# Attention and channel mix on one core: mu by DMA, value weights behind batch 1's loads, more unread matmuls, last tile in halves, new places for the steps

**Chip, cores, metric.** One core of one Trainium2 chip. The metric is the time of one execution in microseconds, device time. A program on one core has no die to compare with, so "fast" only says that no run lay over 1.5% above the fastest of its kernel.

## The reference, cut to what matters

```python
# attention over 32 memory slots; 8 batches, 8 heads, 576 tokens, 64 per head
a = softmax(phi, axis=tokens)
k_m, v_m = a^T k, a^T v                       # per head: 32 x 64
attn = softmax(q k_m^T / 8);  x = attn v_m    # heads side by side: 576 x 512
# channel mix
xk = mu_k * x + (1 - mu_k) * x_prev;  xr = mu_r * x + (1 - mu_r) * x_prev
out = sigmoid(xr @ w_r) * (relu(xk @ w_k) ** 2 @ w_v)
```

Inputs and output are float32. The kernel multiplies in bf16; the load from memory casts.

## The kernel before: what the change touches

The work of a batch is cut into named steps: q0 to q3 transpose queries, k, v and z are the products with exp(phi), nk and nv their norms, s0 to s3 scores, l0 to l3 logs of the denominators, mk and mr the mixing products. Channel mix runs in nine chunks of 512 tokens, 16 groups each: eight of keys, four gates, four of values. A list gives each step a place, counted in groups, and the places settle every engine's order. (A suffix such as +pv names the result buffer that the step borrows; digits after an underscore are only a label.) In the traces an engine's work comes in that order, and a step that waits holds up what stands behind it: in the kernel before TensorE stood idle for 3.09 us until batch 0's keys landed, and for 1.89 us at 50 us until VectorE had weights.

```python
FIRST = {0: [("exp", -36), ("busy16_572686", -36), ("k+pv", -34), ("z", -32), ..., ("mu", -26), ("s1", -25), ...],
         1: [...], 2: [...], 3: [...]}        # later batches: STEADY
ORDER = ('wv', 'phi', 'k', 'q', 'v')          # loads after those of batch 0 and w_k, w_r
# ... cut ...
    mu_row = const.tile([1, 2, Dm], F32, name="mu_row")
    nc.sync.dma_start(out=mu_row[:, 0], in_=moe_mu_k.unsqueeze(0))
    nc.sync.dma_start(out=mu_row[:, 1], in_=moe_mu_r.unsqueeze(0))
# ... cut: the step "mu" ...
        for jj in range(2):                   # mu_row to all partitions, by TensorE
            nc.tensor.matmul(ps[jj * 64:(jj + 1) * 64], lhsT=ones_f, rhs=mu_row...[:, :, :, jj, :], ...)
        for w in range(2):
            nc.vector.tensor_mul(mu_m[:, w, 0], mask, ps[:, w])
            nc.vector.tensor_sub(mu_m[:, w, 1], mask, mu_m[:, w, 0])
# ... cut: a group of values ...
                o = work.tile([128, Dm], F32, name="o", tag="o", bufs=2)
                for fi in range(NF):
                    nc.tensor.matmul(pv, lhsT=st["sq"][:, fi, ts * 128:(ts + 1) * 128],
                                     rhs=wv_sb[:, fi, :], start=(fi == 0), stop=(fi == NF - 1))
                nc.vector.tensor_mul(o, st[ts // 2][:, ts % 2], pv)
                store(o, t0 // 128 + ts)
```

"busy16" is 16 matmuls on zeros whose result nobody reads: they are meant to keep TensorE's clock up. All loads that cast go through one queue, issued by GpSimd, in program order.

The softmax here doesn't subtract the row's maximum and nothing guards it: scores larger than these inputs give would overflow.

## Time and profile before

| | before |
|---|---|
| time, median of 3 runs (range) | 235.5 us (235.37 to 235.9) |
| span of the profiled run | 233.9 us |
| first keys matmul | 25.48 us |
| stretch bound by TensorE's work | from about 76 us to 228.8 us |

The page's engine rows for PE and for its clock. Columns of the first row: busy us, share, instructions; the second row is the granted clock in tenths in 40 slices of 5.8 us.

```profile
PE 215.5 (92%) x1606; PEld 107.6 (46%) x1633; DVE 142.1 (61%) x353; ACT 162.1 (69%) x305; POOL 54.0 (23%) x74
...
PEclk9956799999999999999999999999999999999999
```

### The profile page before, as it was taken

To read this page: it belongs to the slowest core of one execution; us is meant where nothing else is said; L and a number is where in the kernel's file an instruction comes from. 1 tells how busy PE (TensorE), PEld (TensorE's weight loads), DVE (VectorE), ACT (ScalarE), POOL (GpSimd) and SP (SyncE) were. 2 spreads that over 40 slices of the span, in tenths; PEclk is the share of its full clock that TensorE was granted. 3 is DMA by queue.
4 is the path that set the end of the run, shared out by engine and by line. 5 is a ranking of instruction groups with operands and counts; after the bars stand their busy time and mean duration, and the time that the engine had idled before them with its cause. 6 is when DMAs were issued, how large, how long until landed. Compare 5 with 4: busy or idle time off the path is not lost.

```text
span 233.9 us, 4281 instructions
## 1 busy us (share of the span) xinstructions
PE 215.5 (92%) x1606; PEld 107.6 (46%) x1633; DVE 142.1 (61%) x353; ACT 162.1 (69%) x305; POOL 54.0 (23%) x74
## 2 busy tenths in 40 slices
PE   7398798869998999999999999999999999999991
PEld 3234345445435445445544684454444444444440
DVE  3254743387566778588657856786577877525222
ACT  3107478761799595889698959895988865765760
POOL 8672155545524607300810000000000000000000
PEclk9956799999999999999999999999999999999999
DMA  7999999999999999993499400320023033023034
GB/s 141 187 200 206 239 192 231 191 259 216 254 209 163 169 227 258 180 189 129 115 163 211 97 3 0 90 93 0 3 91 90 1 90 93 0 91 90 0 69 113
DMA packets 48633, 31.23 MB, mean 134 GB/s; under 512 B 14826, under 2 KB 42994, under 8 KB 48612
## 3 DMA queue, kind: packets, MB, share of 16 engines
q0 software_dynamic: 41520, 20.91, 63.9%
q1 hardware_dynamic: 6932, 9.78, 14.4%
q8 instruction: 13, 0.21, 0.4%
q10 hardware_dynamic: 160, 0.26, 0.3%
q14 instruction: 8, 0.07, 0.1%
HBM read 38.28 MB, written 9.44 MB: 204 GB/s over the span
## 4 chain that ended last, share of the span: by engine, by line
PE 81%; ACT 5%; DMA 4%; DVE 3%; issue 2%; SPq 1%; POOL 1%; DVEq 0%; POOLq 0%
PE pk L483 25%; PE pv L513 23%; PE pr L497 13%; PE qtps L295 4%; PE kvps L241 4%; DMA q<-in_q_dram 3%; PE scps L309 2%; PE nops L349 2%; PE zps L322 2%; SPq L464 1%; PE mxps L403 1%; DMA out_dram<-o 1%; PE mxps L407 1%; PE zps L251 1%; DVE o L515 1%
## 5 line engine op out<-in xcount | busy, mean ns | idle before, releaser
L483 PE MATMUL pk<-xkT,wk 128*128 128x512 bf16 (+1 forms) x309 | 66.9, 360 | 1.2 <-issue 0.5
L513 PE MATMUL pv<-wv,sq 128*128 128x512 bf16 x280 | 65.1, 379 | 0.6 <-issue 0.2
L487 ACT ACTIVATE rl<-pk 128x512 bf16<-128x512 f32 x72 | 43.1, 601 | 25.4 <-PE pk L483 23.7
L488 DVE TENSOR_TENSOR sq<-rl 128x512 bf16<-128x512 bf16 x72 | 29.9, 423 | 25.9 <-ACT rl L487 25.9
L515 DVE TENSOR_TENSOR o<-sg,pv 128x512 f32<-128x512 f32 x36 | 23.9, 686 | 35.5 <-ACT sg L505 27.8
L483 PEld LDWEIGHTS <-wk 128*128 128x128 bf16 x320 | 29.6, 98 | 28.1 <-issue 1.2
L513 PEld LDWEIGHTS <-sq 128*128 128x128 bf16 x288 | 27.8, 98 | 31.7
L497 PE MATMUL pr<-wr,xrT 128*128 128x512 bf16 x137 | 34.9, 380 | 0.4 <-issue 0.2
L502 ACT ACTIVATE sg<-pr 128x512 f32<-128x512 f32 x36 | 21.7, 604 | 10.5 <-PE pr L497 10.5
L312 ACT ACTIVATE e<-scps 128x288 bf16<-128x288 f32 x32 | 11.7, 431 | 12.2 <-PE scps L309 12.2
L497 PEld LDWEIGHTS <-xrT 128*128 128x128 bf16 x144 | 13.0, 98 | 15.4 <-issue 1.4
L504 ACT ACTIVATE sg<-sg 128x1024 f32<-128x1024 f32 x18 | 19.0, 1057 | 0.6
L505 ACT ACTIVATE sg<-sg 128x1024 f32<-128x1024 f32 x18 | 19.0, 1057 | 0.6
L353 ACT CAST x<-nops 128x288 bf16<-128x288 f32 x48 | 16.6, 413 | 0.0
L374 DVE TENSOR_SCALAR mu_d<-diff,mu 128x576 bf16<-128x576 bf16 x48 | 15.6, 368 | 0.0
L299 DVE COPY qT<-qtps 128x576 bf16<-128x576 bf16 x32 | 12.9, 450 | 4.3 <-PE qtps L295 4.2
L295 PE MATMUL qtps<-identity,q 128*64 128x128 bf16 x320 | 12.9, 233 | 1.9 <-DMA q<-in_q_dram 0.7
L324 ACT ACTIVATE lz<-zps 128x288 f32<-128x288 f32 x32 | 12.0, 415 | 3.8 <-PE zps L322 3.8
L109 POOL DMA_DIRECT2D phm<-in_phi_dram x7 | 6.3, 895 | 36.1 <-ACT em L225 31.6
L241 PE MATMUL kvps<-kv,em 128*64 128x256 bf16 (+1 forms) x200 | 10.8, 255 | 3.2 <-DMA kv<-in_k_dram 3.1
L336 DVE TENSOR_TENSOR atn<-e,lz 128x576 bf16<-128x576 bf16 x16 | 11.9, 753 | 1.9 <-ACT lz L329 1.8
L295 PEld LDWEIGHTS <-q 128*64 128x64 bf16 x320 | 10.4, 116 | 4.8 <-issue 3.0
(70 smaller groups left out, 214.1 us busy)
## 6 DMA issues: line engine op xcount, KB each, us to landing
out_dram<-o SPq DMA_DIRECT2D x38, 128.0 KB, 2.4
kv<-in_k_dram POOLq DMA_DIRECT2D x8, 512.0 KB, 10.4
out_dram<-o SPq DMA_DIRECT2D x16, 256.0 KB, 4.8
phm<-in_phi_dram POOLq DMA_DIRECT2D x7, 512.0 KB, 10.7
q<-in_q_dram POOLq DMA_DIRECT2D x7, 512.0 KB, 11.7
kv<-in_v_dram POOLq DMA_DIRECT2D x7, 512.0 KB, 12.1
wk<-in_moe_w_k_dram POOLq DMA_DIRECT2D x2, 512.0 KB, 9.8
wv<-in_moe_w_v_dram POOLq DMA_DIRECT2D x1, 1024.0 KB, 16.8
```

Of the source, the lines that this page charges most:

```text
L241: nc.tensor.matmul(kvps[jj * 64:(jj + 1) * 64, c], lhsT=heads(j, pr * 64, 64), rhs=kv5[:, parts, 2 * pr:2 * pr + 2, j, :], start=j == 0 an ...
L295: nc.tensor.matmul(ps[i * D:(i + 1) * D, j * 128:(j + 1) * 128], lhsT=q5[:, 2 * pr + i, j, :], rhs=identity, is_transpose=True, start=True ...
L353: nc.scalar.copy(st["x"][:, 2 * c + jj, sl], pss[jj])
L483: nc.tensor.matmul(pk[:, lo:hi], lhsT=wk_sb[:, di, fi * 128:(fi + 1) * 128], rhs=xk_T[:, di, c0:c0 + hi - lo], start=(di == 0), stop=(di = ...
L487: nc.scalar.activation(rl, pk, AF.Relu)
L488: nc.vector.tensor_mul(st["sq"][:, fi, :], rl, rl)
L497: nc.tensor.matmul(pr, lhsT=xr_T[:, di, c0:c0 + 128], rhs=wr_sb[:, di, :], start=(di == 0), stop=(di == ND - 1))
L502: nc.scalar.activation(sg[:, ts % 2], pr, AF.Exp, scale=-1.0)
L504: nc.scalar.activation(sg, sg, AF.Ln, bias=1.0)
L505: nc.scalar.activation(sg, sg, AF.Exp, scale=-1.0)
L513: nc.tensor.matmul(pv, lhsT=st["sq"][:, fi, ts * 128:(ts + 1) * 128], rhs=wv_sb[:, fi, :], start=(fi == 0), stop=(fi == NF - 1))
L515: nc.vector.tensor_mul(o, st[ts // 2][:, ts % 2], pv)
```

## The change

The intent: shorten the way to the first keys matmul (mu by DMA, fillers until the keys land), have batch 1's keys and queries there sooner, and shorten the end. With it came new places for most steps, which its description does not name. The diff, cut to its core:

```diff
-    0: [("exp", -36), ("busy16_572686", -36), ("k+pv", -34), ..., ("mu", -26), ("s1", -25), ...
+    0: [("exp", -58), ("busy23_232748", -54), ("mu", -48), ("k+pv", -47), ("z+pv", -45), ("busy1_400335", -45), ...
     (nearly all places of batches 0 to 3 and some steady ones; 9 fillers in later waits instead of 4)
-ORDER = ('wv', 'phi', 'k', 'q', 'v')
+ORDER = ('phi', 'k', 'q', 'wv', 'v')
-    nc.scalar.preload_act_table_set("natural_log_exp_and_others")      # moved behind the four issues
+    mu_b = const.tile([128, 2, 2, 2 * D], F32, name="mu_b")
+    for w, mu in enumerate((moe_mu_k, moe_mu_r)):
+        for jj in range(2):
+            nc.scalar.dma_start(out=mu_b[jj * 64:(jj + 1) * 64, w],
+                in_=mu.rearrange("(c j x) -> j c x", c=2, j=2)[jj:jj + 1].to_broadcast([64, 2, 2 * D]))
-            nc.tensor.matmul(ps[jj * 64:(jj + 1) * 64], lhsT=ones_f, ...)
-            nc.vector.tensor_mul(mu_m[:, w, 0], mask, ps[:, w])
+            nc.vector.tensor_mul(mu_m[:, w, 0], mask, mu_b[:, w])
-                o = work.tile([128, Dm], F32, name="o", tag="o", bufs=2)
+                o = work.tile([128, Dm], F32, name="o", tag="o", bufs=3)
+                n = 2 if c == NCH - 1 and ts == 3 else 1        # product and store by halves of the columns
```

## The prediction

The table load that part 1 speaks of took 1.28 us from 0.74 us on.

> **What bounds the kernel now.** I read the page's slices first, then stretches of time, then the order of instructions of the first 60 us, then the end. The stretches were cut at every 3.41 us up to 31 us, because the granted clock turned out to flip on that grid. The columns are: stretch, its length, busy us of TensorE's matmuls, its weight loads, VectorE, ScalarE and GpSimd (instructions in brackets), granted clock, DMA share, GB/s.
>
> ```profile
> 4.10:7.51 3.41, 2.10 (x10) 0.89 (x9) 0.98 (x13) 1.40 (x2) 3.33 (x7) 1.00 1.44 183
> 7.51:10.92 3.41, 1.08 (x30) 0.90 (x29) 0.47 (x3) 0.00 (x0) 1.79 (x3) 0.99 1.62 188
> 10.92:14.33 3.41, 3.26 (x27) 1.61 (x27) 1.50 (x6) 0.00 (x0) 2.63 (x4) 0.50 1.56 192
> 17.74:21.15 3.41, 3.39 (x26) 1.38 (x26) 0.74 (x2) 2.75 (x8) 0.88 (x1) 0.51 1.25 206
> 21.15:24.56 3.41, 1.73 (x40) 1.14 (x38) 3.09 (x8) 1.70 (x5) 1.43 (x2) 0.99 1.24 207
> 24.56:27.97 3.41, 3.08 (x25) 1.32 (x21) 2.28 (x7) 1.76 (x4) 0.14 (x1) 0.51 1.19 263
> 36.00:48.00 12.00, 10.71 (x130) 6.08 (x130) 4.52 (x12) 9.20 (x17) 6.29 (x8) 1.00 1.51 212
> 48.00:60.00 12.00, 9.68 (x138) 6.07 (x135) 10.19 (x28) 5.13 (x12) 6.31 (x8) 1.00 1.42 239
> 76.00:150.00 74.00, 73.26 (x577) 39.12 (x583) 53.29 (x129) 58.84 (x118) 16.23 (x21) 1.00 0.85 141
> 150.00:222.00 72.00, 71.47 (x396) 32.95 (x403) 44.79 (x100) 54.41 (x94) 0.00 (x0) 1.00 0.19 56
> ```
>
> From 76 us to the last matmul (228.8 us) TensorE is idle for 0.74 + 0.53 + 0.08 = 1.35 us at full clock, and eight 512-column matmuls take 1.73 us, 216 ns each. No part of the change removes work there, so those 153 us stay. All that can be won lies in four places: the time until the first key matmul, which comes at 25.48 us; the half clock around it; idle TensorE between 28 and 76 us (0.05 + 1.29 + 2.32 + 0.77 = 4.4 us); and the 5.1 us after 228.8 us.
>
> The way to 25.48 us is a chain of latencies, shown by these lines of the timeline (start, duration, engine, line, what; in brackets the idle time before):
>
> ```profile
> 1.19 5.01 PE L193 MATMUL idle<-zeros 128*128 128x512 bf16 x16 [1.19 <-DVE zeros L137]
> 9.29 0.75 PE L241 MATMUL kvps<-kv,em 128*64 128x128 bf16 x20 [3.09 <-DMA kv<-in_k_dram]
> 11.07 1.35 PE L295 MATMUL qtps<-identity,q 128*64 128x128 bf16 x20 [0.69 <-DMA q<-in_q_dram]
> 12.88 1.97 PE L203 MATMUL psmu<-mu_row,ones_f 1*64 1x512 f32 x4
> 14.78 0.45 PE L309 MATMUL scps<-qT,kmT 128*64 128x288 bf16 x2
> 20.14 0.69 ACT L329 ACTIVATE lz<-lz 128x576 f32<-128x576 f32 x1
> 25.48 1.49 PE L483 MATMUL pk<-xkT,wk 128*128 128x512 bf16 x3 [0.33 <-DVE xkT L412]
> 50.07 0.30 PE L403 MATMUL mxps<-atn,vm 64*128 64x288 bf16 x2 [1.89 <-DVE atn L336]
> 229.28 0.69 DVE L515 TENSOR_TENSOR o<-sg,pv 128x512 f32<-128x512 f32 x1 [0.42 <-DMA out_dram<-o]
> ```
>
> Keys land at 9.2 us, the first queries at 11.0. The broadcast of mu on TensorE occupies it from 12.88 to 14.85 us, just where the first score matmul (14.78) could go. The first reciprocal is at 20.14. The last output product has 0.42 us of wait for a store to free one of two buffers.
>
> [...] with clock shares solved for the instant of change, the flips lie at 10.84, 21.08, 24.52 and 27.92 us, multiples of 3.41 us apart, and the filler matmuls go from 430 to 216 ns apart after 4.1 us. [...] the stretch 10.92 to 14.33 is busy 3.26 of 3.41 us, with 22 transposes and four one-row matmuls in it, and the next one was not granted full clock. [...]
>
> **Part 1: mu by DMA.** Removed: 1.97 us of TensorE, which delays the first scores, and the 0.47 us that the third query transpose waits for a buffer which mu held. Moved: the four mask operations (0.42 us each, 1.7 us together) from 14.9 to 16.5 us on VectorE into its idle time before the keys (7 to 10.4 us). Added: four issues on ScalarE's queue, at the 0.25 to 0.56 us of the small issues on SP some 1.8 us; the table load then ends near 4 us, and phi lands at 5.3: hidden. Also added: 4 x 128 rows of 512 B = 512 packets. The page's queue table gives 63.9% of 16 x 233.9 us for 41520 packets, 58 ns each, so 512 of them cost 16 engines 1.8 us. [...] I estimate that keys and queries come 0.5 us later, not 1.8.
>
> Now the chain. VectorE's order becomes: first query copy, keys' norm, second copy, key transpose copy. From queries at 11.07: transposes at full clock 0.47 (ten later in the trace), copy 0.45 to 12.0, norm 0.61 to 12.65, copy to 13.1, key copy 0.28 to 13.4; first scores at 13.4 instead of 14.78. Then, with the durations of the trace: exponentials 0.41 + 0.35 to 14.55; third query pair 14.55 to 15.0 and fourth 15.55 to 16.0 on VectorE, two logs meanwhile; third and fourth exponential 16.4 to 17.1; first reciprocal at 17.1 instead of 20.14, because mu's masks and the half clock no longer sit between. Weights (0.75) to 18.6, masked values (four, 1.13) to 19.75, second weights to 20.5, last mixing matmuls about 21, their copies on two engines to 22.3; first keys matmul about 21.9, as its first pieces start before the last copy. With 0.5 us of later keys: 22.4. **Gain: 25.48 - 22.4 = 3.1 us**; I count 2.9.
>
> **Part 2: unread matmuls.** 23 instead of 16 before the keys: 7 x 0.216 = 1.5 us more, so they end near 7.7 us, where TensorE is idle until 9.3. In all 9 other ones instead of 4 lie in later waits. They cost nothing there, and should hold the clock. Before, from 25.48 to 27.97 TensorE worked at half rate, a loss of 1.2 us. [...] **Expected gain: 0.45 us**, out of 1.2 won or 0.8 lost.
>
> **Part 3: value weights behind phi, keys and queries of batch 1.** The value weights write 1 MB; at the measured 200 GB/s that is 5.2 us. Batch 1's phi, keys and queries land 5 us sooner, the value weights later. They landed at 12.04 + 16.8 = 28.8 us and were first read at 41.3, so there was room. In the new order they land near 37 us (where batch 1's queries landed before), and the first value matmul comes at 22.4 + 12 groups of 0.863 + mixing 0.7 + batch 1's keys, sums, queries and scores 3.7 = 37.2 us: just in time. Without this part the earlier start would run into late queries. Batch 1's scores now stand one group earlier, so that a value group lies between scores and weights; of the waits (1.89 for weights, 0.46, 0.57) I expect half to go. **Gain: 0.8 us** net of some wait on the value weights.
>
> **Part 4: last tile in halves, third output buffer.** The matmul work is the same. The last gate's chain on ScalarE still ends at 227.08 + 1.06 = 228.14 us; then 0.69 for the tile before, then two halves at an estimated 0.38: 229.65 instead of 229.97. The last store moves half the bytes, but sits behind another issue of about 0.5 us on its queue. **Gain: 0.4 us.**
>
> Sum: 2.9 + 0.45 + 0.8 + 0.4 = 4.55; I take off a little for the new order of the steady steps, which has nothing to win: 235.5 - 4.3 = **231.2 us**, 1.8% faster.
>
> **Rivals.** A: the broadcast delays keys. For it: the keys are the first thing that TensorE waits for (3.1 us)[...]. [...] If its 1.8 us came in full, 1.3 us more is lost: 232.5. B: a new wait on the value weights or on phi takes back the head start[...]. For it: my two times differ by 0.2 us. Against: the swap takes out exactly the 5 us item in front. It would give 233. C: the clock fails, half rate from 22.4 to 27.9, 2.7 us lost instead of 1.2: 233. D: [...] most of batch 1's waits go: 229.5.
>
> **Range and chances.** A, B and C are each perhaps one in four and rarely together; D is one in five. I put 229.2 to 233.4 at 8 in 10. The border of 2% is 230.8, only 0.4 below my number: faster 0.42, same 0.56, slower 0.02, since a loss of 4.7 us would need a stall that nothing in the profile suggests.
>
> **What would show it.** Right: first scores near 13.9 us, first keys matmul at 22 to 23, clock 1.00 from there on, idle TensorE between 28 and 76 us below 4 us, the last matmul near 224.5, the last output product not waiting for a store, and the steady stretch as long as before. Wrong: keys' first matmul after 10.2 us (A); a wait of value matmuls on a DMA near 38 us or of ScalarE on phi near 28 (B); clock 0.5 in the stretch after the first keys matmul (C); or a change of some us in the steady stretch, which would break the premise that it is bound by TensorE's work alone.

## The result

The changed kernel takes 232.68 us (median of 4 runs, 232.32 to 233.43), the kernel before 235.44 us in the same rounds. The ratio is 0.9887, interval 0.9855 to 0.9919: the same at a threshold of 2%, though clear of 1. Ratios here are the mean time of one kernel's fast runs over that of the other's of the same rounds, so not quite the ratio of the medians.

The same two rows of the page, after:

```profile
PE 217.9 (94%) x1649; PEld 108.4 (47%) x1649; DVE 142.6 (62%) x353; ACT 161.2 (70%) x305; POOL 54.1 (23%) x74
...
PEclk9958999999999999999999999999999999999998
```

The change adds 16 matmuls by count of its parts (12 fillers and 8 for the halves, less 4 records of mu), and 1649 less 16 is 1633. So the profile of before lacks 27 matmul records, and a missing record looks like an idle TensorE.

The order of the first 64 us, after (timeline: start, duration, engine, line, what; idle time before in brackets), with the lines that answer to those of before:

```profile
10.11 0.87 PE L238 MATMUL kvps<-kv,em 128*64 128x128 bf16 x20 [1.60 <-DMA kv<-in_k_dram]
...
12.05 0.75 PE L292 MATMUL qtps<-identity,q 128*64 128x128 bf16 x10 [0.50 <-DMA q<-in_q_dram]
...
14.77 0.69 PE L306 MATMUL scps<-qT,kmT 128*64 128x288 bf16 x4 [0.43 <-DVE kmT L282]
...
23.25 2.96 PE L480 MATMUL pk<-xkT,wk 128*128 128x512 bf16 x12
...
50.92 0.81 PE L292 MATMUL qtps<-identity,q 128*64 128x128 bf16 x22 [0.44 <-DMA q<-in_q_dram]
...
63.53 0.68 PE L292 MATMUL qtps<-identity,q 128*64 128x128 bf16 x10 [0.50 <-DMA q<-in_q_dram]
```

Keys come 0.82 us later than before and queries 0.98 us; yet the keys matmuls start 2.2 us earlier. New are waits of TensorE on queries at 50 and 63 us.

And the stretches (length, busy us of matmuls, weight loads, VectorE, ScalarE, GpSimd, clock, DMA share, GB/s), cut where this run's clock flipped:

```profile
8.37:11.78 3.41, 1.59 (x32) 1.14 (x32) 1.99 (x6) 0.00 (x0) 1.42 (x2) 1.00 1.65 188
11.78:15.20 3.42, 2.72 (x27) 1.63 (x29) 1.63 (x5) 0.00 (x0) 2.40 (x4) 0.50 1.58 191
15.20:18.61 3.41, 3.41 (x31) 1.65 (x26) 0.92 (x2) 1.47 (x4) 2.47 (x3) 0.50 1.27 209
18.61:22.02 3.41, 3.18 (x40) 1.47 (x39) 1.88 (x6) 2.63 (x7) 0.69 (x1) 1.00 1.24 204
...
76.00:150.00 74.00, 74.00 (x583) 38.92 (x578) 54.07 (x128) 61.44 (x122) 14.86 (x19) 1.00 0.88 148
150.00:222.00 72.00, 72.00 (x404) 32.80 (x402) 44.75 (x99) 52.21 (x90) 0.00 (x0) 1.00 0.18 52
```

The clock still falls at 11.8 us, and the stretch from 76 us has no idle time at all.

Where the time came from is read best from milestones: the start of the relu behind a given group of keys, and the end of ScalarE's last gate instruction, from the two traces.

| milestone | before | after | gained |
|---|---|---|---|
| chunk 0, first keys | 27.01 | 24.52 | 2.5 |
| chunk 0, third keys | 30.38 | 26.25 | 4.1 |
| chunk 0, last keys | 35.47 | 32.75 | 2.7 |
| chunk 1, first keys | 60.24 | 56.91 | 3.3 |
| chunk 1, last keys | 68.57 | 66.09 | 2.5 |
| chunk 2, first keys | 86.26 | 83.78 | 2.5 |
| chunk 8, fifth keys | 215.87 | 213.38 | 2.5 |
| last gate ends | 228.13 | 225.65 | 2.5 |
| span | 233.85 | 231.62 | 2.2 |

(The 4.1 is mostly a change of order: before ran two mixing steps between these groups.) From chunk 2 on the difference stands at 2.49 us. So the steady places do nothing, all was won before 66 us, 0.85 us of it was given back between 57 and 66 us, and 0.25 at the end. The chain that ended last shows the giving back; here its pieces around 60 us (start, us, what):

```profile
50.55 12.94 DMA q<-in_q_dram
63.49 0.04 issue
63.53 0.41 PE qtps L292 x8
```

Before, this chain ran mainly over TensorE and ScalarE there; now it runs 12.94 us through the load of batch 3's queries.

### The profile page after: what moved, and what is told of

Same layout as the page of the kernel before. It is cut to its first block, busy times and chain, and to the rows that moved or that the text cites. A ratio compares the mean times of both kernels' runs of the same rounds, so it can differ in the third digit from the quotient of the medians.

```text
span 231.6 us, 4343 instructions
## 1 busy us (share of the span) xinstructions
PE 217.9 (94%) x1649; PEld 108.4 (47%) x1649; DVE 142.6 (62%) x353; ACT 161.2 (70%) x305; POOL 54.1 (23%) x74
## 4 chain that ended last, share of the span: by engine, by line
PE 78%; DMA 10%; ACT 5%; DVE 3%; issue 1%; POOL 1%; DVEq 0%; POOLq 0%
PE pk L480 25%; PE pv L513 24%; PE pr L494 13%; DMA q<-in_q_dram 10%; PE qtps L292 4%; PE kvps L238 3%; PE nops L346 2%; PE scps L306 2%; PE zps L319 1%; ACT sg L501 1%; ACT sg L502 1%; DVE atn L333 1%; ACT sg L499 1%; PE zps L248 1%; ACT e L309 1%
## 5 line engine op out<-in xcount | busy, mean ns | idle before, releaser
L513 PE MATMUL pv<-wv,sq 128*128 128x512 bf16 (+1 forms) x296 | 66.2, 373 | 0.0
L515 DVE TENSOR_TENSOR o<-sg,pv 128x512 f32<-128x512 f32 (+1 forms) x37 | 23.9, 672 | 32.5 <-ACT sg L502 25.2
L513 PEld LDWEIGHTS <-sq 128*128 128x128 bf16 x296 | 28.6, 98 | 32.3 <-issue 0.7
L494 PE MATMUL pr<-wr,xrT 128*128 128x512 bf16 x144 | 35.5, 380 | 0.0
L292 PE MATMUL qtps<-identity,q 128*64 128x128 bf16 x320 | 13.4, 233 | 1.5 <-DMA q<-in_q_dram 1.4
L321 ACT ACTIVATE lz<-zps 128x288 f32<-128x288 f32 x32 | 11.4, 410 | 3.2 <-PE zps L319 3.2
```

What stands on the lines that cost most here:

```text
L292: nc.tensor.matmul(ps[i * D:(i + 1) * D, j * 128:(j + 1) * 128], lhsT=q5[:, 2 * pr + i, j, :], rhs=identity, is_transpose=True, start=True ...
L494: nc.tensor.matmul(pr, lhsT=xr_T[:, di, c0:c0 + 128], rhs=wr_sb[:, di, :], start=(di == 0), stop=(di == ND - 1))
L513: nc.tensor.matmul(pv[:, cols], lhsT=st["sq"][:, fi, ts * 128:(ts + 1) * 128], rhs=wv_sb[:, fi, cols], start=(fi == 0), stop=(fi == NF - 1))
L515: nc.vector.tensor_mul(o[:, cols], st[ts // 2][:, ts % 2, cols], pv[:, cols])
```

## The experiments

**Theory 1.** The head start runs into the stream of loads, which delivers batch 2 at about 50 to 54 us and batch 3's queries at 62 to 63 us whatever TensorE does; and mu's broadcast puts this stream back. **Rival.** ScalarE and VectorE cap the stages from 45 to 76 us, and the waits on loads are incidental. All twelve kernels gave correct results. The kernel before had a median of 235.8 to 236.1 us beside these runs. Four kernels ran per group, in three groups. The changed kernel itself was repeated only in the third, so the other two groups are compared with it across groups.

### 1. mu by TensorE again, at its new place

```diff
-    (four nc.scalar.dma_start into mu_b)
+    (mu_row, ones_f and the two matmuls of the kernel before, in the step "mu", still ahead of the keys)
```

> The changed kernel with one part undone: mu is broadcast by TensorE again, but at its new early place, ahead of the keys. Theory 1 (the stream of loads is the cap: the 512 packets of the broadcast put every later load back by about 1 us, and TensorE meets the stream again at the queries of batches 2 and 3): keys land at 9.3 instead of 10.1 us, the queries of batch 3 near 62.5 instead of 63.5, and the whole is 0.8 to 1.2 us faster than the changed kernel, 231.5 to 231.9. Rival (the cap between 45 and 76 us is ScalarE's and VectorE's work, the wait on queries is incidental): keys come as early, the end gains at most 0.3 us, 232.4 or more.

231.58 us (231.21 to 233.06), ratio 0.9849 [0.9807, 0.989]: by the medians about 1.1 us faster than the changed kernel, by the ratios of its two measurements 0.4 to 0.9 us, with overlapping intervals. Its timeline at the keys:

```profile
8.98 0.22 PE L199 MATMUL psmu<-identf,mu 8*128 8x8 f32 x1
9.14 1.07 PE L204 MATMUL psmu<-mu_row,ones_f 1*64 1x512 f32 x4
10.14 0.75 PE L242 MATMUL kvps<-kv,em 128*64 128x128 bf16 x20
...
49.39 1.23 PE L296 MATMUL qtps<-identity,q 128*64 128x128 bf16 x30 [1.84 <-DMA q<-in_q_dram]
```

At this place the broadcast takes 1.07 us. Keys landed at 8.60 us and were first read at 10.14, behind the fillers and the broadcast; the changed kernel, where they landed at 10.07, read them at 10.11. Over the fourteen profiles they landed at 8.6 to 9.9 us in the six without the DMA broadcast and at 9.4 to 11.1 in the eight with it. In this run the clock stayed full, and keys matmuls began at 20.66 us. That lead is the clock's and not mu's: number 8, with mu by TensorE too but the clock at half from 12.3 to 19.2 us, began them at 23.08, the changed kernel, at half from 11.8 to 18.6, at 23.25. The clock is also a rival for the gain in time, since four of these six runs have a mean clock of 0.993 or more and the ten of the changed kernel 0.981 to 0.991. Against it: the one run here at 0.979 has a span of 230.0 us, under all ten of those (230.5 to 232.2), and number 4 shows that a full clock alone does not reach the end. Even so TensorE waited 1.8 us for batch 2's queries, as Theory 1 has it. Batch 3's queries landed at 61.86 instead of 63.49 us.

### 2. The last tile whole, three buffers kept

```diff
-                n = 2 if c == NCH - 1 and ts == 3 else 1
+                n = 1
```

> The changed kernel with the last tile stored whole, its third output buffer kept. Theory: halves bring nothing, since the last product is held back by ScalarE's gate either way and the third store issue on each queue starts 0.56 us after the product: the last product ends at the same time within 0.1 us, the stores start at once, and the end is 0.2 to 0.5 us earlier than in the changed kernel. Rival (the smaller transfers pay for the issues): 0.3 us later.

232.43 us (232.04 to 233.39), ratio 0.9871 [0.9838, 0.9905]. A difference of 0.25 us from the changed kernel is under what these runs resolve; the traces do resolve it. First the changed kernel's end, then this one's:

```profile
225.68 1.35 DVE L515 TENSOR_TENSOR o<-sg,pv 128x512 f32<-128x512 f32 x3 [3.84 <-ACT sg L502]
226.40 1.75 SPq L461 DMA_DIRECT2D out_dram<-o  x3
226.40 2.04 ACTq L461 DMA_DIRECT2D out_dram<-o  x3
```

```profile
224.92 1.33 DVE L515 TENSOR_TENSOR o<-sg,pv 128x512 f32<-128x512 f32 x2 [3.85 <-ACT sg L502]
225.64 1.11 SPq L461 DMA_DIRECT2D out_dram<-o  x2
225.64 1.38 ACTq L461 DMA_DIRECT2D out_dram<-o  x2
```

Both wait for the same gate, and the products take 1.35 and 1.33 us. Halves add a third issue to each queue: the last issue starts 0.86 us after the last product instead of 0.03. From the end of the last gate to the end of the span the six profiles with halves and the DMA broadcast take 5.94 to 6.00 us, this one 5.34, the kernel before 5.72. So, in the changed kernel, the halves lost about 0.6. The third buffer won nothing that shows: numbers 5 and 11, with the tile whole and two buffers, took 5.36 and 5.43 us, and their last product waited for no store. The waits of 0.42 us before and 0.23 in number 6 stand in the two profiles in which an issue of an earlier store took 1.82 and 1.62 us on SyncE instead of 0.55; why it did is open. Without the broadcast of mu by DMA the halves cost less: number 1 took 5.59 us for this stretch, the whole-tile numbers 8, 9 and 11 took 5.43 to 5.48, so 0.11 to 0.16. Why four early issues on ScalarE's queue should matter at the end stays open.

### 3. Value weights first again

```diff
-ORDER = ('phi', 'k', 'q', 'wv', 'v')
+ORDER = ('wv', 'phi', 'k', 'q', 'v')
```

> The changed kernel with the value weights loaded first again. Theory 1: queries of batch 1 land near 37.9 us instead of 32.4 and TensorE waits for them 1.5 to 2.5 us near 36 us; the slack of the later stages (0.9 us) takes a part back; end 0.7 to 1.5 us later than the changed kernel. Rival (the order of loads matters nothing, since the total is what caps): within 0.3 us.

233.38 us (232.86 to 235.86), ratio 0.9916 [0.9872, 0.996]: 0.45 to 0.7 us slower than the changed kernel's two medians, within the intervals of each other. The wait is there, on keys rather than queries:

```profile
PE kvps L238 <- DMA kv<-in_k_dram: 1.5, 1, 1.5
```

Keys of batch 1 landed at 34.5 instead of 29.3 us. With them late, TensorE came later to batch 2's queries and waited no more there; that is where most of the 1.5 us went: its trace reaches the first keys of chunk 2 at 83.72 us, the changed kernel's at 83.78. (Its clock was at half for 3.4 us instead of 6.8, so the two are not quite alike.)

### 4. 31 unread matmuls

```diff
-("busy23_232748", -54)
+("busy31_232748", -54)
```

> The changed kernel with 31 instead of 23 unread matmuls ahead of the keys, so that TensorE is busy to about 9.9 us. [...] the clock now stays full from 4 us on and the first keys matmul comes 1 to 1.6 us sooner (21.7 to 22.3 us). Theory 1 (loads are the cap) then has the end gain at most 0.4 us, with longer waits on queries near 50 and 63 us. Rival (the head start passes through to the end): 1 us or more faster than the changed kernel.

233.41 us (232.68 to 234.06), ratio 0.9905 [0.9871, 0.9939]. This is the sharpest test: the first keys matmul came at 21.04 us, 2.2 us earlier than in the changed kernel, and the end no sooner. The wait of this profile from 45 to 60 us, and the stretches around it:

```profile
PE qtps L292 <- DMA q<-in_q_dram: 2.1, 1, 2.1
```

```profile
46.00:50.20 4.20, 2.12 (x31) 1.15 (x29) 3.01 (x7) 2.24 (x5) 1.58 (x2) 1.00 1.48 221
50.20:53.60 3.40, 3.40 (x35) 1.88 (x30) 1.37 (x3) 0.00 (x0) 1.57 (x2) 0.50 1.41 273
```

The queries landed at 49.96 us, as ever, and behind the wait the clock was 0.50 from 50.2 to 53.6 us. The clock differs from run to run, though. Its six runs had mean clocks from 0.980 to 1.000, and the spans do not follow them: 231.8 us at 0.980, 231.5 at 1.000. In these runs start and clock hardly matter once the loads set the pace.

### 5 and 6. Parts 1 and 3 alone, on the kernel before

```diff
 b_mu:    the four DMA issues in place of mu_row and its matmuls; lists, ORDER and the end as before
 b_order: -ORDER = ('wv', 'phi', 'k', 'q', 'v')
          +ORDER = ('phi', 'k', 'q', 'wv', 'v')
```

> The kernel before with part 1 alone: mu by DMA, all else as it was. Keys land near 10.1 instead of 9.25 us, the two mu matmul rows of 1.97 us are gone from the place ahead of the first scores. Theory (the broadcast is paid in the stream of loads): first keys matmul at 24.3 to 25.2 instead of 25.48, and the end within 0.6 us of the kernel before, since all later loads come about 1 us later. Rival (what left TensorE is won in full): 1.2 us or more faster than before.

> The kernel before with part 3 alone: value weights behind phi, keys and queries of batch 1. In the kernel before, batch 1's keys and queries were there 3.4 us before use, and the value weights 12 us. So nothing waits for them either way: within 0.4 us of the kernel before; value weights land near 37 us. Rival (order matters by itself): faster by 0.8 us or more.

Part 1 alone: 236.48 us, ratio 1.0056 [1.001, 1.0103], slower than before. The first keys matmul came 1.25 us earlier (24.23 us), but at the first keys of chunk 1 this kernel was 0.66 us behind. It waited 0.5 us for queries and had a clock of 0.50 from 50.2 to 53.6 us, where the kernel before had 1.00, in this profile:

```profile
46.00:50.20 4.20, 1.79 (x46) 1.34 (x42) 3.43 (x9) 3.07 (x7) 1.77 (x3) 1.00 1.48 224
50.20:53.60 3.40, 3.40 (x27) 1.58 (x22) 1.31 (x3) 0.52 (x2) 1.37 (x2) 0.50 1.35 284
```

Part 3 alone: 235.76 us, ratio 0.9997 [0.9965, 1.003]: nothing, as expected of a load that nobody waits for.

### 7. 31 unread matmuls, queries of batches 2 and 3 placed later

```diff
-    2: [("q3", -2), ("q0", -2), ("q1+pv", -2), ...
+    2: [("q3", -1), ("q0", -1), ("q1+pv", -1), ...
-    3: [("q0", -11), ...
+    3: [("q0", -9), ...
```

> The changed kernel with 31 unread matmuls, and with the query transposes of batches 2 and 3 placed one or two groups later in TensorE's order, so that value and key groups run while the queries land. Theory 1 (the head start was lost in the wait on batch 2's queries[...]): the wait of 2.1 us at 48 us falls to under 0.5 us, and the end is 1.2 to 2.2 us faster than with 31 unread matmuls alone. Rival (the stages after it are capped by ScalarE or VectorE): the wait moves to another instruction and the end gains at most 0.4 us.

232.83 us (232.36 to 234.01), ratio 0.9886 [0.9848, 0.9924]. That is 0.6 us faster than number 4 (in another group, with overlapping intervals), half of the least that I expected. I had taken queries for the whole of the cap. They are only the next item of the stream, as the waits of this profile show:

```profile
PE kvps L238 <- DMA kv<-in_v_dram: 2.1, 1, 2.1
```

The same 2.1 us, now on batch 2's values, which landed at 54.5 us. The wait on queries there was gone. That the wait would move was the rival's forecast; but it moved to another load, not to ScalarE or VectorE, so the miss speaks for Theory 1. The clock stayed full in this profile although the wait is as long as number 4's.

### 8. First version meant to beat both

```diff
 number 1 (mu by TensorE), number 2 (n = 1) and the two lines of number 7 together, 23 unread matmuls
```

> A version meant to beat both: the changed kernel with mu by TensorE ahead of the keys, the last tile stored whole, and the later query transposes of batches 2 and 3. From the single results (1.1 us, 0.2 us and up to 0.9 us): 230.0 to 231.0 us. If the wait on queries was not the cap, 231.2 or more.

231.15 us (230.99 to 232.97), ratio 0.9821 [0.9784, 0.9859]: just over the 230.0 to 231.0 that I expected, and unclear at the threshold of 2%.

### 9. Second version: all of batch 2 later

```diff
 number 8, and
-    2: ("kv", -1), ("q2", -1), ("z", -1), ("nk", -1), ("nv", -1), ("tk", 0), ("s2+pv", 1), ("s0", 1), ("s1", 1), ("s3", 1)
+    2: ("kv", 1), ("q2", 0), ("z", 1), ("nk", 1), ("nv", 1), ("tk", 2), ("s2+pv", 2), ("s0", 2), ("s1", 2), ("s3", 2)
-    0: ("mr2+pv", 2), ("mr0+pk", 2), ("mr1", 2)
+    0: ("mr2+pv", 2), ("mr0", 3), ("mr1+pv", 4)
```

> Mu by TensorE ahead of the keys, last tile whole, and now all of batch 2's early work (queries and also keys and values) one or two groups later, and the three mixing steps of the receptance spread over three groups. With 31 unread matmuls and later queries alone the wait moved from queries to values of batch 2 (2.1 us at 52.4 us). If the stream of loads is the cap, no wait over 0.6 us on a load is left between 40 and 70 us and the end is 0.4 to 1.2 us faster than the version with later queries alone (231.15): 230.0 to 230.8. If another engine is the cap, 231.0 or more.

230.50 us (229.27 to 232.61), ratio 0.9769 [0.9723, 0.9816]: 2.3% under the kernel before, but unclear at the threshold of 2%, since the interval reaches 0.9816. It is faster than the changed kernel (232.93 us in the same group, ratio 0.9868 [0.9832, 0.9904]); against number 8, in another group, the intervals overlap. Its longest waits of TensorE from 45 to 60 us:

```profile
PE scps L310 <- DVE kmT L286: 1.1, 1, 1.1
PE mxps L404 <- DVE vm L385: 0.9, 1, 0.9
```

No load is among them. The profiled run was not one of the better ones (span 229.7, others down to 227.5). At 7.8 us it waited 1.7 us for the 2 KB row of mu, which another run had in time; issuing mu's rows ahead of phi would be the next thing to try and was not tried.

### 10. Fillers undone

```diff
-("busy23_232748", -54) and nine unread matmuls in six later places
+("busy16_232748", -54) and none later
```

> The changed kernel with part 2 undone: 16 unread matmuls at the start, none later. The clock is half for longer around 11 to 25 us and the first keys matmul comes 0 to 1.5 us later. Theory 1 (the stream caps at batch 2's and 3's loads): the end moves less than the start, within 0.6 us of the changed kernel. Rival (the fillers win what they save): 1 us or more slower than the changed kernel.

233.49 us (232.64 to 234.81), ratio 0.99 [0.986, 0.9939], against 232.93 for the changed kernel in the same group: 0.56 us, with overlapping intervals. The first keys matmul came at 23.64 us.

### 11. The new places alone, on the kernel before

```diff
 STEADY and FIRST of the changed kernel (fillers included); mu by TensorE, value weights first,
 last tile whole with two buffers, as before
```

> The kernel before with the two lists of places alone (with the fillers in them): mu by TensorE, value weights first, last tile whole with two buffers. If the new places carry the gain, and not the three parts that the change names, this is faster than before by 2.4 to 3.6 us: 232.2 to 233.4. If the parts carry it, it is within 1 us of before.

231.85 us (231.11 to 233.04), ratio 0.9822 [0.978, 0.9864]. **The places alone win more than the whole change**, whose ratio in the same group is 0.9868 [0.9832, 0.9904]. The two intervals overlap a little, but five of the six runs here are under 232.5 us and five of the six of the changed kernel over it. It is also more than I expected of the places (232.2 to 233.4). First keys matmul at 21.02 us, last gate at 224.72 us, 3.4 us before that of the kernel before. It waited 2.4 us at 31.3 us, which the profile lays to ScalarE; batch 1's keys landed at 33.62 us, just as the wait ended (33.75), so it was the load.

### 12. The changed kernel again

> The changed kernel once more, on the chip that ran the experiments, for direct comparison: 232.3 to 233.1 us by the earlier measurement.

232.93 us (232.28 to 234.0), ratio 0.9868 [0.9832, 0.9904].

### The stream of loads in five kernels

Landing times in us, from the traces:

| load | before | changed | no. 1 | no. 4 | no. 9 |
|---|---|---|---|---|---|
| keys, batch 0 | 9.25 | 10.07 | 8.60 | 9.41 | 8.97 |
| queries, batch 1 | 36.38 | 32.35 | 31.41 | 32.08 | 31.47 |
| value weights | 28.82 | 37.85 | 36.91 | 37.59 | 36.98 |
| queries, batch 2 | 49.46 | 50.02 | 49.35 | 49.96 | 49.45 |
| values, batch 2 | 52.93 | 53.58 | 53.18 | 53.72 | 52.42 |
| queries, batch 3 | 61.71 | 63.49 | 61.86 | 63.05 | 61.57 |
| first keys matmul | 25.48 | 23.25 | 20.66 | 21.04 | 22.13 |

The first keys matmul varies by 4.8 us, batch 2's queries by 0.7.

The traces of the kernel before and of the changed one show a pattern in this pace. In both, seven or eight of GpSimd's loads are in flight whenever it has issued one between 25 and 66 us (47 issues in the two), never more than eight among all 68 of a run, and each of the 60 behind the first eight is issued only after the load eight before it has landed: 0.28 us after it at the earliest, 0.53 to 0.55 us after it in 19 of the 47. The load of batch 3's queries (issued at 49.99 and 50.55 us) follows the landing of batch 2's (49.46 and 50.02) by 0.53 us in both. So the issues go with GpSimd's own earlier loads, though the profile lays this wait to TensorE in the changed kernel. Where the eight come from, the runs do not show.

## Why the prediction was right, and where its steps were wrong

The range (229.2 to 233.4) and the likeliest class (same, 0.56) held; the number, 231.2, was 1.5 us too low. It stood for the wrong reasons in part, and that it fell into the range is partly luck: the start gave 2.2 us where 2.9 were counted, and where parts 3 and 4 counted gains, 0.85 us went back from 57 to 66 us and 0.25 at the end. Of its signs, the first scores came at 14.77 us instead of 13.9, and the first matmul on keys at 10.11, just under the 10.2 that was to show rival A, which held all the same.

- **The premise** that the steady stretch gives nothing: right, to 0.01 us from chunk 2 on. Its 1.35 us of idle time there were missing records, not idle time.
- **Part 1**, "Gain: 25.48 - 22.4 = 3.1 us": the start came at 23.25 (2.2 us won), and not by the DMA. The step that failed is "Removed: 1.97 us of TensorE", which took the removal for the gain. With the same matmuls at the new place the start was as early (23.08 us in number 8, at a like clock), and the DMA version alone started 1.25 us earlier but ended later than before (number 5). The chain was also worked out at full clock from 11 us on; it ran at half clock from 11.8 to 18.6 us. The delay of the keys was put at 0.5 us and was 0.82 (0.40 in the repeat, landing at 9.65). In its place the gain belongs to the new lists as a whole: which of their places carries it, mu's, batch 0's or batch 1's, was not separated.
- **Part 2**: fillers did not bridge to the keys. They ended at 8.2 us, and keys came at 10.1. Clock was full from the first keys matmul on (1.00 from 18.6 to 230.2 us), as the step had it. The step was reckoned by the busy time of TensorE in stretches of 3.41 us; the traces do not bear it out (last section). Undoing all fillers costs 0.56 us by the medians, with overlapping intervals.
- **Part 3**, "Gain: 0.8 us": the mechanism was right and the value weights came just in time, with no wait on them (37.85 us landed, first read at 39.8). The size failed because of rival B, in another place than I had put it. I looked for the wait at the value weights and at phi, and it came at the queries of batches 2 and 3, 0.44 us and 0.50 us in the timeline. The 0.6 us that batch 1 won by 57 us went back by 66 us. What the order of loads is worth is not shown: alone it gave nothing (number 6), undoing it cost 0.45 to 0.7 us within overlapping intervals (number 3), and number 11 did without it.
- **Part 4**, "Gain: 0.4 us": lost 0.25 in the profiles. It failed at "sits behind another issue of about 0.5 us on its queue", which I had noted and not charged: the halves cost about 0.6. And the wait of 0.42 us for a store was no lasting cost of two buffers, since numbers 5 and 11 have two and no such wait.
- **Rival A** was right in kind: keys came 0.8 us later than before and 1.5 later than in number 1, and the later loads of the table 0.4 to 1.6 us later than in number 1. Taking the broadcast away won 1.1 us by the medians (with overlapping intervals), and adding it to the kernel before made that slower, clear of 1 (number 5). Its packets can be counted in the page's queue table, ScalarE's queue before, after and in number 2:

```profile
q10 hardware_dynamic: 160, 0.26, 0.3%
```

```profile
q10 hardware_dynamic: 816, 0.52, 0.9%
```

```profile
q10 hardware_dynamic: 736, 0.52, 0.9%
```

Of the 656 more packets 80 belong to the halved stores, for number 2 has the broadcast and the whole tile. The other 576 took 0.6% of 16 engines' 231.6 us, 1.4 us each, near the 1.8 us estimated. I had let two thirds of it hide; it did not hide. The column of the DMA share adds the packets' times over 16 engines and reads up to 1.65 in the stretches above (8.37 to 11.78 us, changed), and no view says what its most would be.

What stays open: whether the stream (227 GB/s over all queues from 25 to 66 us before, 218 in the changed kernel) would move faster with more than eight loads in flight. No run changed the size or number of its transfers.

## What to carry to other kernels

Ask of a head start where the next load lands: a start that comes 2.2 us earlier is worth nothing if the third batch's queries land at 50 us either way (number 4). Moving a small job off the busiest engine was a loss here, because the engine had room for it in a wait (in number 8 the broadcast ended 0.33 us before the keys landed), and the job's new carrier is the one that sets the pace. Test the parts of a change singly: here the unnamed part, the new order, won more than the sum, and two of the named ones lost: mu by DMA in the times, the halves in the traces.

## What else the traces show

- Clock and gaps. Here the clock fell to 0.50 at 11.8 us after a gap of 1.6 us ahead of the keys, in a stretch busy 1.59 of 3.41 us (changed kernel), and at 50.2 us after one of 2.1 us (number 4). After a gap as long it stayed at 1.00 in number 7. The busy time of TensorE alone gives no rule either: a stretch of 3.41 us busy for 2.17 us (before, 4.03 to 7.44 us) was followed by a clock of 1.00, one busy for 2.72 us (changed kernel, 11.78 to 15.20 us) by 0.50. What decides is not shown.
- The first rise to full clock, read from the spacing of the fillers (427 ns, then 216), came at 4.1 us in the profile of before and at 5.0 in that of the changed kernel. Kernels with fillers are therefore compared over several runs.
- Beside the stream of loads, mu's 64 KB broadcasts took 4.9 to 7.7 us from issue to landing in the changed kernel, and a 2 KB row held up number 9 until 9.5 us, after an issue near 3 us.
- The profile of before lacked 27 of 1633 matmul records, and they read as idle time.
- A third issue on each queue at the end moved the last issue from 0.03 (number 2) to 0.86 us (changed kernel) after the last product.
